# Fewer accumulator groups, evictions written ahead of weight conversions, and Fourier low parts on VectorE

## The chip, the cores and the metric

The kernel runs on one core of one Trainium2 chip. The metric is the device time of one execution in microseconds (us). TensorE (PE) multiplies, and its results land in accumulators (PSUM banks); VectorE (DVE), ScalarE (ACT) and GpSimd (POOL) do elementwise work; SyncE (SP) only issues DMAs.

## The reference

Three parts run one after the other on two batches of 768 tokens with 512 channels: a block attention with decay, a mixer MLP (token MLP, then channel MLP), and a Fourier block with a second channel MLP. All is float32.

```
x  = attention(q, k, v, lam)                      # per head, decay lam
xt = x.transpose(0, 2, 1)
u  = x + (relu(xt @ w_tok1) @ w_tok2).transpose(0, 2, 1)
x  = u + relu(u @ w_ch1) @ w_ch2                  # channel MLP, 512 -> 1536 -> 512   (m = 0)
u  = x + real(fft(fft(x, axis=1), axis=2))
un = (u - mean(u)) / sqrt(var(u) + 1e-6)
out = u + relu(un @ m_w_ch1) @ m_w_ch2            # second channel MLP, 512 -> 2048 -> 512   (m = 1)
```

The weights arrive as 64-bit floats, which the kernel reads as pairs of 32-bit integer words and turns into float32 itself.

## The kernel before

**Products.** Each float32 operand is split into a high part and a low part (what the high part leaves over), and `mm3` (L114 to L118) makes a product of three matmuls: high times high, high times low, low times high. So a product shows as a turn of L116, L117, L118. A high part is an ACT copy, a low part is a subtraction on DVE or POOL.

**Steps of the two channel MLPs.** `run` (L949) goes through a list `todo` of hidden tiles, one a step. `first(u)` makes the tile's first product into one bank `ph`: 12 matmuls of 384 columns. `relu_split` (L484) then makes its high part on ACT (L485) and its low part on DVE (L486), named `hid`. One step later `second` multiplies `hid` by the second weight and adds it to a group of accumulators `ac`: four banks for m = 0 (12 matmuls of 384 columns), three for m = 1 (9 of 512). So on PE `first` of step i stands ahead of `second` of step i - 1, and a `hid` has the time of one `first` to get ready before PE stands still. In names such as ph_1_0_6 the digits are batch, column half and hidden tile.

**Groups.** `units(m, blocks, last_f)` (L676) orders the hidden tiles: for each (tiles, batch) the two column halves, and in a half all tiles of the list. At the last tile of a half the group ends: DVE adds each bank to the residual, four times 128x384 at L494 for m = 0 (`xT`), three times 128x512 at L502 for m = 1 (`u`). Until that is done the next group's `second` can't write the banks. `G1` holds the twelve tiles of m = 0 in four threes.

**Weights.** `convert(n)` (L260) takes n turns on a stream of jobs. A job of two-word weights (512 KB load on SP, L184) takes one ACT pass (L203), four DVE word operations (L222, L223, L225, L226), and then either an ACT copy and a POOL subtraction into one of 16 places of converted weights (L252, L253), or, for a job of kind "ahead" (raw names end in a), a store to a scratch in memory (L234), from where the weight comes back later as float32 (256 KB load, names end in s). A converted place is taken only when one is free (`room`); three buffers hold raw words, three hold the results. `TURNS` says how many turns are taken in a step (1 where it says nothing), and `TURNS_7` how many in the last part.

**Fourier.** Its pieces (`fourier_ab`, `fourier_d`, sums, y, gather, columns, rows, mid, and `norm`) are called from within the steps at half-steps given in `WHEN`. `fourier_y` computes six arrays y (L775 to L795), and `emit` splits each: the unscaled four with an ACT copy (L760) and a POOL subtraction (L761), the two scaled ones on ACT and, put off to the end of the piece in the list `late`, on DVE (L767). They go into `ya` and `yb`, which the column transforms (`pm`) and `fourier_mid` (`pz`, L811 and L812) multiply.

**The last part.** The rest of the second MLP is done by `seven` (L596), which makes two by two blocks of products from seven (`pa`, `pb`, `pc`), with sums of inputs and weights; `between` takes conversion turns and `second_of` between its products.

**Order.** The order on PE and SP is the one that the code is written in. On DVE, ACT and POOL a scheduler orders the instructions from what is written and what waits for what.

## Time and profile before

| | us |
| --- | --- |
| median of 3 runs (632.94 to 635.19) | 634.0 |
| the profiled execution, its own time | 631.0 |
| span of its trace | 629.2 |
| TensorE busy | 600.1 |
| VectorE busy | 465.8 |
| ScalarE busy | 236.5 |
| GpSimd busy | 157.1 |

The profiled execution is one more run beside the three. The trace gives the start and length of each instruction and what its engine waited for last. Times along the trace are counted from the start of the span. The m = 0 MLP runs alone from about 129 us to 264 us, the Fourier transform of the first batch between its last steps to 312 us, then the second batch's with the second MLP to 440 us, and the last part follows.

### The profile page before, as it was taken

Reading aid. Unit: us, or ns where it says so; the run is one execution under the profiler, and the core shown is the slowest. Engines: PE = TensorE matmul, PEld = TensorE weight load, DVE = VectorE, ACT = ScalarE, POOL = GpSimd, SP = SyncE. Lnnn points to the kernel's source line nnn. Section 1 sums busy time; section 2 is a strip of 40 time slices with the busy share of each in tenths; the row PEclk is TensorE's granted clock in tenths of the full one; section 3 lists DMA queues with packets and bytes.
Section 4 is the critical chain, followed back from the end, with each engine's and each line's share of the span. In section 5 each row is a group of like instructions: output and inputs, shape, how many; then the busy total and the mean of one; then the engine's idle time right before and its main releaser. Section 6 shows DMA issues by size and latency. Waiting matters only on the chain. (4 is left out here: it accounts for less than half of the span.)

```text
span 629.2 us, 9565 instructions
## 1 busy us (share of the span) xinstructions
PE 600.1 (95%) x3624; PEld 547.3 (87%) x3624; DVE 465.8 (74%) x894; ACT 236.5 (38%) x480; POOL 157.1 (25%) x127
## 2 busy tenths in 40 slices
PE   9999899999899998999899999999999998999997
PEld 7677699899799997999899899888889977999996
DVE  6799899999978689448786885885697699335335
ACT  2575654534323324134434451323443442221110
POOL 5254223324201401014523440024402332110000
PEclk9999999999999999999999999999999999999999
DMA  8955334414574586201102001003203424000005
GB/s 286 400 219 168 125 101 129 144 68 145 168 251 125 177 262 195 102 0 45 58 18 83 26 10 35 17 1 84 83 2 124 161 68 134 1 0 1 0 1 200
DMA packets 25069, 66.35 MB, mean 105 GB/s; under 512 B 2872, under 2 KB 4032, under 8 KB 25024
## 3 DMA queue, kind: packets, MB, share of 16 engines
q1 hardware_dynamic: 24736, 65.62, 31.5%
q8 instruction: 28, 0.46, 0.3%
q10 hardware_dynamic: 288, 0.14, 0.1%
q14 instruction: 17, 0.14, 0.1%
HBM read 55.51 MB, written 10.23 MB: 104 GB/s over the span
## 5 line engine op out<-in xcount | busy, mean ns | idle before, releaser
L118 PE MATMUL ac<-w_b,hid 128*128 128x512 f32 x192 | 75.9, 395 | 0.3 <-DVE hid L486 0.3
L117 PE MATMUL ac<-w_b,hid 128*128 128x512 f32 x192 | 75.7, 394 | 0.0
L116 PE MATMUL ac<-w_b,hid 128*128 128x512 f32 x192 | 74.9, 390 | 0.0
L116 PE MATMUL ac<-hid,w_b 128*128 128x384 f32 x192 | 64.9, 338 | 4.4 <-DVE xT L494 4.3
L117 PE MATMUL ac<-hid,w_b 128*128 128x384 f32 x192 | 64.8, 338 | 2.7 <-DVE hid L486 2.7
L118 PE MATMUL ph<-uh,w_a 128*128 128x384 f32 x192 | 64.4, 335 | 0.5 <-POOL w_a L253 0.5
L116 PE MATMUL ph<-uh,w_a 128*128 128x384 f32 x192 | 64.6, 337 | 0.0
L118 PE MATMUL ac<-hid,w_b 128*128 128x384 f32 x192 | 64.3, 335 | 0.0
L117 PE MATMUL ph<-uh,w_a 128*128 128x384 f32 x192 | 64.2, 334 | 0.0
L486 DVE SCALAR_TENSOR_TENSOR hid<-ph,hid 128x384 fp32r<-128x384 f32 x68 | 37.5, 551 | 34.4 <-ACT hid L485 34.3
L485 ACT ACTIVATE hid<-ph 128x384 fp32r<-128x384 f32 x68 | 33.0, 486 | 72.2 <-PE ph L118 72.1
L253 POOL TENSOR_TENSOR w_a<-m_a,w_a 128x512 fp32r<-128x512 f32 x17 | 25.1, 1478 | 91.6 <-ACT w_a L252 56.1
L118 PEld LDWEIGHTS ac<-w_b,hid 128*128 128x128 f32 x192 | 36.0, 188 | 8.4 <-DVE hid L486 0.7
L117 PEld LDWEIGHTS ac<-w_b,hid 128*128 128x128 f32 x192 | 36.0, 188 | 6.1
L116 PEld LDWEIGHTS ac<-w_b,hid 128*128 128x128 f32 x192 | 36.1, 188 | 5.8
L116 PEld LDWEIGHTS ac<-hid,w_b 128*128 128x128 f32 x192 | 36.0, 188 | 5.8 <-ACT hid L485 2.4
L117 PEld LDWEIGHTS ac<-hid,w_b 128*128 128x128 f32 x192 | 36.1, 188 | 4.1 <-DVE hid L486 3.9
L253 POOL TENSOR_TENSOR w_b<-m_b,w_b 128x512 fp32r<-128x512 f32 x17 | 24.0, 1410 | 62.2 <-ACT w_b L252 32.5
L118 PEld LDWEIGHTS ph<-uh,w_a 128*128 128x128 f32 x192 | 36.0, 188 | 0.8 <-POOL w_a L253 0.8
L117 PEld LDWEIGHTS ph<-uh,w_a 128*128 128x128 f32 x192 | 36.1, 188 | 0.1
L116 PEld LDWEIGHTS ph<-uh,w_a 128*128 128x128 f32 x192 | 36.1, 188 | 0.1
L118 PEld LDWEIGHTS ac<-hid,w_b 128*128 128x128 f32 x192 | 36.0, 188 | 0.0
(466 smaller groups left out, 1509.6 us busy)
## 6 DMA issues: line engine op xcount, KB each, us to landing
qkv<-qkv SPq DMA_DIRECT2D x7, 768.0 KB, 8.1
single_scratch<-m_a SPq DMA_DIRECT2D x16, 256.0 KB, 4.2
qkv<-qkv SPq DMA_DIRECT2D x10, 384.0 KB, 5.8
kp<-kT SPq DMA_DIRECT2D x8, 384.0 KB, 6.3
single_scratch<-m_b SPq DMA_DIRECT2D x11, 256.0 KB, 4.4
out<-u SPq DMA_DIRECT2D x11, 256.0 KB, 2.0
raw_t_0d<-w_tok SPq DMA_DIRECT2D x2, 384.0 KB, 7.5
raw_t_1d<-w_tok SPq DMA_DIRECT2D x2, 384.0 KB, 3.1
```

The lines of the kernel that those rows point to most:

```text
L116: nc.tensor.matmul(ps, wt[0], xt[0], start=first, stop=False, **kw)
L117: nc.tensor.matmul(ps, wt[0], xt[1], start=False, stop=False, **kw)
L118: nc.tensor.matmul(ps, wt[1], xt[0], start=False, stop=last, **kw)
L253: nc.gpsimd.tensor_tensor(out=t[:, 1, :n], in0=src, in1=f32(t[:, 0, :n]), op=ALU.subtract)
L485: nc.scalar.activation(hi, ps, AF.Relu)
L486: stt(out=lo, in0=ps, scalar=0.0, in1=f32(hi), op0=ALU.max, op1=ALU.subtract)
```

## The change

1. The lists of hidden tiles are cut into fewer, longer groups. For m = 0 there were seven entries with 14 group ends (56 additions at L494): tiles G1[0] for batch 0, then for batch 1, G1[1] for batch 0, then for batch 1, G1[2] with G1[3] for batch 0, G1[2] for batch 1, G1[3] for batch 1. Now there are five entries with 10 ends (40 additions). For m = 1, batch 0, two entries become one: 4 ends with 12 additions become 2 with 6. The number and kind of matmuls stay.
2. At a step whose `second` ends a group, `convert` is called behind `second` and no longer ahead of it, in `run` and in `between`.
3. The low parts of the four unscaled Fourier arrays of each batch (8 operations of 128x512) go from POOL to DVE and are put off to the end of their piece.
4. `TURNS` has other values: no conversion in steps 39 to 42, and two turns at more of the other steps. The first piece of the Fourier transform of batch 0 comes two steps later (half-step 67, not 63).

```diff
-WHEN = ((63, 71, 77, 73, 74, 77, 74, 77, 77, 79, 80, 81, 85, 83, 86, 85, 87, 84, 88, 90, 92, 91, 94, 97, 99),
+WHEN = ((67, 71, 77, 73, 74, 77, 74, 77, 77, 79, 80, 81, 85, 83, 86, 85, 87, 84, 88, 90, 92, 91, 94, 97, 99),
...
-TURNS = {3: 0, 5: 0, 20: 3, 21: 3, 22: 3, 23: 2, 24: 2, 26: 2, 28: 2, 41: 0, 42: 0, 45: 0, 48: 0, 49: 0, 62: 0, 65: 0}
+TURNS = {3: 0, 5: 0, 16: 2, 18: 2, 20: 2, 22: 2, 24: 2, 26: 2, 28: 2, 29: 2, 39: 0, 40: 0, 41: 0, 42: 0, 43: 2, 45: 2, 46: 2,
+         48: 0, 49: 0, 62: 0, 65: 0}
...
                 nc.scalar.activation(yh[:, 0, :], src, AF.Copy)
-                nc.gpsimd.tensor_tensor(out=yh[:, 1, :], in0=src, in1=f32(yh[:, 0, :]), op=ALU.subtract)
+                late.append(lambda: tt(out=yh[:, 1, :], in0=src, in1=f32(yh[:, 0, :]), op=ALU.subtract))
...
-    todo = units(0, [(G1[0], 0), (G1[0], 1), (G1[1], 0), (G1[1], 1), (G1[2] + G1[3], 0), (G1[2], 1), (G1[3], 1)], 11)
-    todo += units(1, [(G1[0], 0), (G1[1], 0)], 15)
+    todo = units(0, [(G1[0], 0), (G1[0] + G1[1], 1), (G1[1] + G1[2], 0), (G1[3], 0), (G1[2] + G1[3], 1)], 11)
+    todo += units(1, [(G1[0] + G1[1], 0)], 15)
...
-            convert(TURNS.get(i, 1))
+
+            ends = i > 0 and todo[i - 1][1] is not None and todo[i - 1][4] == todo[i - 1][1][-1]
+            if not ends:
+                convert(TURNS.get(i, 1))
             for fn, args in side.get(2 * i, []):
                 fn(*args)
             if i > 0:
                 second(todo[i - 1])
+            if ends:
+                convert(TURNS.get(i, 1))
...
-            convert(TURNS_7[j] * (i + 1) // 4 - TURNS_7[j] * i // 4)
-            if pend:
-                pend.pop(0)()
+            turns = TURNS_7[j] * (i + 1) // 4 - TURNS_7[j] * i // 4
+            ends, fn = pend.pop(0) if pend else (False, lambda: None)
+            if ends:
+                fn()
+            convert(turns)
+            if not ends:
+                fn()
```

How the instructions stand on VectorE around the first group end inside the m = 0 stretch; before (the end belongs to batch 1, column half 0; `m_a_9` and `m_b_9` are weights whose words are being converted):

```order
L225 SCALAR_TENSOR_TENSOR m_b_8_1818<-raw_b_8d,m_b_8_1818 128x512
L222 TENSOR_SCALAR m_a_9_1857<-m_a_9_1857 128x512
L226 SCALAR_TENSOR_TENSOR m_b_8_1818<-raw_b_8d,m_b_8_1818 128x512
L486 SCALAR_TENSOR_TENSOR hid_1_1_0_1595<-ph_1_1_0_1582,hid_1_1_0_1595 128x384
L494 TENSOR_TENSOR xT_178<-ac_1_0_0_0_1527,xT_178 128x384
L494 TENSOR_TENSOR xT_178<-ac_1_0_0_1_1528,xT_178 128x384
L494 TENSOR_TENSOR xT_178<-ac_1_0_0_2_1529,xT_178 128x384
L494 TENSOR_TENSOR xT_178<-ac_1_0_0_3_1530,xT_178 128x384
L223 TENSOR_SCALAR m_a_9_1857<-m_a_9_1857 128x512
L222 TENSOR_SCALAR m_b_9_1900<-m_b_9_1900 128x512
L225 SCALAR_TENSOR_TENSOR m_a_9_1857<-raw_a_9d,m_a_9_1857 128x512
L223 TENSOR_SCALAR m_b_9_1900<-m_b_9_1900 128x512
```

and after (the same group now ends three tiles later):

```order
L227 SCALAR_TENSOR_TENSOR m_a_9_1886<-raw_a_9d,m_a_9_1886 128x512
L487 SCALAR_TENSOR_TENSOR hid_1_0_4_1634<-ph_1_0_4_1621,hid_1_0_4_1634 128x384
L487 SCALAR_TENSOR_TENSOR hid_1_0_5_1673<-ph_1_0_5_1660,hid_1_0_5_1673 128x384
L487 SCALAR_TENSOR_TENSOR hid_1_1_0_1712<-ph_1_1_0_1699,hid_1_1_0_1712 128x384
L495 TENSOR_TENSOR xT_178<-ac_1_0_0_0_1527,xT_178 128x384
L495 TENSOR_TENSOR xT_178<-ac_1_0_0_1_1528,xT_178 128x384
L495 TENSOR_TENSOR xT_178<-ac_1_0_0_2_1529,xT_178 128x384
L495 TENSOR_TENSOR xT_178<-ac_1_0_0_3_1530,xT_178 128x384
L223 TENSOR_SCALAR m_b_9_1897<-m_b_9_1897 128x512
L224 TENSOR_SCALAR m_b_9_1897<-m_b_9_1897 128x512
```

The four additions stood directly behind the `hid` before too; what is new is that no word operation stands among the two `hid` ahead of them.

On VectorE in `fourier_y` of batch 0, before:

```order
L783 TENSOR_TENSOR y_3_3048<-q_2591,y_0_3036 128x512
L787 TENSOR_TENSOR y_4_3069<-ra_1_2974,ra_2_2975 128x512
L789 SCALAR_TENSOR_TENSOR y_5_3071<-y_4_3069,ra_0_2973 128x512
L767 TENSOR_TENSOR ya_3034<-y_1s,ya_3034 128x512
L792 TENSOR_TENSOR y_6_3075<-ra_1_2974,ra_2_2975 128x512
L486 SCALAR_TENSOR_TENSOR hid_1_1_8_3099<-ph_1_1_8_3086,hid_1_1_8_3099 128x384
L795 TENSOR_TENSOR y_7_3081<-ra_0_2973,y_4_3069 128x512
L767 TENSOR_TENSOR yb_3035<-y_3s,yb_3035 128x512
```

and after:

```order
L784 TENSOR_TENSOR y_3_3005<-q_2627,y_0_2994 128x512
L762 TENSOR_TENSOR ya_2992<-y_1_2996,ya_2992 128x512
L788 TENSOR_TENSOR y_4_3023<-ra_1_2940,ra_2_2941 128x512
L487 SCALAR_TENSOR_TENSOR hid_1_0_10_2989<-ph_1_0_10_2976,hid_1_0_10_2989 128x384
L768 TENSOR_TENSOR ya_2992<-y_1s,ya_2992 128x512
L762 TENSOR_TENSOR yb_2993<-y_3_3005,yb_2993 128x512
L790 SCALAR_TENSOR_TENSOR y_5_3025<-y_4_3023,ra_0_2939 128x512
L793 TENSOR_TENSOR y_6_3028<-ra_1_2940,ra_2_2941 128x512
L796 TENSOR_TENSOR y_7_3034<-ra_0_2939,y_4_3023 128x512
L762 TENSOR_TENSOR ya_2992<-y_5_3025,ya_2992 128x512
L487 SCALAR_TENSOR_TENSOR hid_1_0_11_3053<-ph_1_0_11_3040,hid_1_0_11_3053 128x384
```

Two of the four low parts per batch (L762) show here among the y; POOL has no instruction between the additions of the batch's `fourier_ab` and its gather any more (before it had the four low parts and five weight conversions there).

A fifth thing follows from the new turns. One pair of weights of the second MLP, a_10 and b_10, is no longer turned to float32 ahead of time. In the last part it is loaded as two-word weights (512 KB, raw_a_10d and raw_b_10d) instead of as float32 (256 KB, raw_a_10s and raw_b_10s), and its word operations stand there. VectorE at the first block of seven (number 2; `u_1_2` is made from the product `pb_2`, `hid_2_11` from `pa_2`), before:

```order
L486 SCALAR_TENSOR_TENSOR hid_1_1_3_4549<-ph_1_1_3_4536,hid_1_1_3_4549 128x384
L613 TENSOR_TENSOR u_1_2_4589<-pb_2_4582,m_1_2_4580 128x384
L486 SCALAR_TENSOR_TENSOR hid_2_11_4606<-pa_2_4573,hid_2_11_4606 128x384
L619 TENSOR_TENSOR v_1_2_4615<-pb_2_4582,m_1_2_4580 128x384
L567 TENSOR_TENSOR x_0_0_4659<-un_0_3389 128x384
```

and after:

```order
L614 TENSOR_TENSOR u_1_2_4527<-pb_2_4520,m_1_2_4518 128x384
L223 TENSOR_SCALAR m_a_10_4713<-m_a_10_4713 128x512
L224 TENSOR_SCALAR m_a_10_4713<-m_a_10_4713 128x512
L226 SCALAR_TENSOR_TENSOR m_a_10_4713<-raw_a_10d,m_a_10_4713 128x512
L227 SCALAR_TENSOR_TENSOR m_a_10_4713<-raw_a_10d,m_a_10_4713 128x512
L487 SCALAR_TENSOR_TENSOR hid_2_11_4544<-pa_2_4511,hid_2_11_4544 128x384
L620 TENSOR_TENSOR v_1_2_4553<-pb_2_4520,m_1_2_4518 128x384
```

The four word operations of a_10 now stand ahead of `hid_2_11` on the engine.

## Rows read from the trace of the kernel before

**Rows 1.** The page: busy us of each engine, share of the span, instructions.
```profile
PE 600.1 (95%) x3624; PEld 547.3 (87%) x3624; DVE 465.8 (74%) x894; ACT 236.5 (38%) x480; POOL 157.1 (25%) x127
```

**Rows 2.** Timeline of PE: start us, us, instruction, [idle before <-what ended it].
```profile
129.16 0.34 PE L116 MATMUL ph<-uh,w_a 128*128 128x384 f32 x1
...
137.49 0.33 PE L116 MATMUL ph<-uh,w_a 128*128 128x384 f32 x1
...
204.04 0.41 PE L116 MATMUL ac<-hid,w_b 128*128 128x384 f32 x1 [0.86 <-DVE xT L494]
...
263.58 0.33 PE L116 MATMUL ph<-uh,w_a 128*128 128x384 f32 x1
```

**Rows 3.** Waits of PE, 129 to 264 us: total us, times, longest us.
```profile
PE ac L116 <- DVE xT L494: 4.3, 4, 1.6
PE ac L117 <- DVE hid L486: 2.7, 3, 1.3
```

**Rows 4.** Timeline of DVE around the group end at 148 us.
```profile
144.42 0.41 DVE L222 TENSOR_SCALAR m_b<-m_b 128x512 f32<-128x512 f32 x1
...
145.33 0.69 DVE L225 SCALAR_TENSOR_TENSOR m_b<-raw_b_8d,m_b 128x512 uint32<-128x512 uint32 x1
145.94 1.54 DVE L222 TENSOR_SCALAR m_a<-m_a 128x512 f32<-128x512 f32 x1
...
148.00 0.55 DVE L486 SCALAR_TENSOR_TENSOR hid<-ph,hid 128x384 fp32r<-128x384 f32 x1
148.47 1.94 DVE L494 TENSOR_TENSOR xT<-ac,xT 128x384 f32<-128x384 f32 x4
```

**Rows 5.** Timeline of POOL around the same group end.
```profile
145.91 1.29 POOL L253 TENSOR_TENSOR w_a<-m_a,w_a 128x512 fp32r<-128x512 f32 x1 [3.03 <-ACT w_a L252]
```

**Rows 6.** Timeline of SP's queue, 215 to 250 us: first and last of ten loads.
```profile
217.81 0.33 SPq L184 DMA_DIRECT2D raw_a_6a<-m_ch  x1
...
242.39 0.33 SPq L184 DMA_DIRECT2D raw_b_10a<-m_ch  x1
```

**Rows 7.** Waits of PE, 264 to 312 us.
```profile
PE pm L117 <- DVE ya L767: 1.6, 1, 1.6
PE pz L811 <- ACT at L841: 1.6, 1, 1.6
```

**Rows 8.** Timeline of DVE in fourier_y of batch 0.
```profile
292.95 1.79 DVE L787 TENSOR_TENSOR y<-ra,ra 128x512 f32<-128x512 f32 x1
295.92 1.77 DVE L789 SCALAR_TENSOR_TENSOR y<-y,ra 128x512 f32<-128x512 f32 x1 [1.18 <-POOL ya L761]
297.61 1.75 DVE L767 TENSOR_TENSOR ya<-y_1s,ya 128x512 fp32r<-128x512 f32 x1
```

**Rows 9.** Waits of PE, 312 to 440 us.
```profile
PE pq L116 <- DVE u L867: 0.6, 1, 0.6
...
PE pn L901 <- DVE unf L892: 0.4, 1, 0.4
```

**Rows 10.** Timeline of DVE in the normalization of batch 1.
```profile
394.55 0.68 DVE L502 TENSOR_TENSOR u<-ac,u 128x512 f32<-128x512 f32 x1
```

**Rows 11.** Timeline of DVE in the last part, blocks 2 and 3.
```profile
446.22 0.56 DVE L613 TENSOR_TENSOR u<-pb,m 128x384 f32<-128x384 f32 x1 [2.54 <-PE pb L118]
449.88 0.56 DVE L486 SCALAR_TENSOR_TENSOR hid<-pa,hid 128x384 fp32r<-128x384 f32 x1 [3.10 <-ACT hid L485]
...
477.37 0.56 DVE L486 SCALAR_TENSOR_TENSOR hid<-pa,hid 128x384 fp32r<-128x384 f32 x1 [2.88 <-ACT hid L485]
```

**Rows 12.** Timeline of SP's queue, block 2.
```profile
444.48 0.32 SPq L180 DMA_DIRECT2D raw_a_10s<-single_scratch  x1
```

**Rows 13.** DMA issues, 440 to 530 us: count, KB each, median us to landing.
```profile
raw_b_11d<-m_ch SPq DMA_DIRECT2D x1, 512.0 KB, 3.5
...
raw_a_10s<-single_scratch SPq DMA_DIRECT2D x1, 256.0 KB, 2.6
```

**Rows 14.** Waits of PE, 440 to 530 us.
```profile
PE pc L116 <- DVE hid L486: 1.2, 2, 1.0
```

More of the change, by code (lines that the diff above doesn't have):

```diff
@@ L1013, in body @@
             input_sums_last(1, k)
-        pend = [lambda: second(todo[-1])]
+        pend = [(False, lambda: second(todo[-1]))]
         place = {"i": 0}
@@ L1033, in body @@
             else:
-                pend.extend([lambda x=x: second_of(*x) for x in todo_])
+                pend.extend([(x[4], lambda x=x: second_of(*x)) for x in todo_])
             if j < 2:
```

## The prediction

> **What bounds the kernel now.** I read the page's busy times first: TensorE is at work in 600.1 us, 95% of the span [rows 1], and the change leaves its matmuls as they are. So what it can win is where TensorE stands still, and what it can lose is a new stop. I looked for the stops stage by stage.
>
> In the m = 0 MLP the timeline gives the length of an undisturbed step: two steps from 129.16 to 137.49 us, so 4.165 us each [rows 2]. The thirty steps from 129.16 to 263.58 us took 134.42 us and should have taken 30 x 4.165 = 124.95: 9.5 us are lost. The list of waits of that stretch names 4.3 us behind the additions of group ends (L494) and 2.7 us behind low parts of hidden tiles (L486) [rows 3], 7.0 in all. The other 2.5 are restarts and stops too short for the list, so a listed us stands for 9.5 / 7.0 = 1.35 lost ones, a factor that I use below. Both waits are on VectorE, which runs late here. The reader sees why in the 148 us rows [rows 4]: word operations stand up to the hidden tile's low part at 148.00, the first two of them run at full speed, and one that should take 0.41 takes 1.54, because the POOL subtraction that starts at 145.91 runs beside it [rows 4, 5]: 1.1 us for one such meeting. Then four additions take 1.94 more.
>
> In the Fourier transform of batch 0 TensorE waits twice for 1.6 us [rows 7]. VectorE stands behind a POOL low part (1.18 idle before 295.92), and its own operations there take 1.75 to 1.79 instead of 0.69 [rows 4, 8].
>
> **m = 0, steps 6 to 35 (term A).** Ends of groups in this stretch go from 8 to 6, since the ends after steps 9, 15 and 21 go and one after step 33 comes. Two ends less are two times 1.94 us of VectorE [rows 4]; more matters what stands around them. Counted in the order of the new kernel, no word operation stands in the two steps ahead of the end at 12 (the fence in the section on the change shows it) and none in steps 24 to 27, so these ends meet a VectorE without a backlog. Those at 30 and 33 have 19 word operations in three steps and then 13. A job's four cost 1.52 us for the first three (144.42 to 145.94) and 0.61 for the fourth, taken as the third's pitch, so 2.13 or 0.53 each [rows 4]. 19 x 0.53 and three low parts of 0.47 (148.00 to 148.47) make 11.5 of the 12.5 us of three steps: no backlog either.
>
> What is left is steps 14 to 23, which take 61 word operations now and one end (at 18). That is 61 x 0.53 + 10 x 0.47 + 1.94 = 39.0 us of 41.65. The nearest stretch before is steps 13 to 21: 41 word operations and three ends, 41 x 0.53 + 9 x 0.47 + 3 x 1.94 = 31.8 of 37.5, and its largest stop is the one at 204.04, 0.86 idle [rows 2], about 1.2 lost. The new stretch leaves 2.7 us of spare time where that one had 5.7. Loads and the buffers of results may set the pace as well: ten loads of such weights were issued between 217.81 and 242.39, 24.58 / 9 = 2.73 us a job [rows 6], and 61 operations are 15.25 jobs, so 41.6 us. It just fits. A hidden tile's low part can be ready some 1.2 us after its product (an ACT pass, taken as 0.6, and its own 0.55 [rows 4]) and is asked for 4.2 us, one step, later, so 3.0 us of lateness cost nothing (an estimate from these). I keep 2.5 us of the 9.5, double the old stretch's stop, and take **A = -7.0**. Ends: -9.3, if only a short stop stays; -3.5, if the full 3 us of missing spare time are lost behind the end and again behind POOL meetings of 1.1 us.
>
> The second edit, evictions ahead of conversions, I cost at nothing: the additions already followed the low part at once (148.00, then 148.47 [rows 4]), and the order shows no other place for them.
>
> **Fourier of batch 0 (term B).** The two waits of 1.6 [rows 7] are 3.2 x 1.35 = 4.3 us. POOL leaves the chain, so the 1.18 idle and the stretching by 1.1 of some four operations (292.95, 295.92, 297.61 and the next [rows 8]) go: 5.6 us off a chain that was late by 1.6 at `pm` and, on top of that, by 1.6 at `pz`. VectorE takes four low parts more, each at most 0.69 like the word operation at 145.33 [rows 4], 2.8 us, of which two stand ahead of the last array for `pm`. In addition the end after step 39 is gone, whose four additions took 1.94 together. 5.6 - 2.8 + 1.9 is more than the 3.2 needed, so both stops go: **B = -4.3**, between -3.2 (bare waits) and, in a rival, nothing. Batch 1 has no such stop, and its four low parts (2.8 us) lie beside full steps: 0.
>
> **Second MLP (term C).** The end after step 45 is gone, whose 1.94 us stood ahead of the chain to `u` (L867), for which `pq` waits 0.6; and the three additions of 0.68 (the last at 394.55 [rows 10]) no longer stand in the chain to `unf`, for which `pn` waits 0.4 [rows 9]. 1.0 x 1.35 = 1.4 at most, 0 at least; **C = -1.0**.
>
> **a_10 and b_10 (term E, a cost).** In block 2 VectorE now has the four word operations of a_10 ahead of `hid_2_11`. The load's issue stood at 444.48 [rows 12] and stays there; 512 KB land in 3.5 us where 256 KB took 2.6 [rows 13], so at 448.0. The ACT pass, taken as 0.6 us, ends at 448.6, the four operations 2.13 later at 450.7, and the low part starts there instead of at 449.88 [rows 11]. TensorE waits for just this low part already (`pc` behind `hid`, 1.2 us in two waits [rows 14]), so all is passed on: +0.8. POOL's subtraction of a sum of weights falls there, and one meeting costs 1.1: **E = +1.9**. Upper end +3.5, with a second meeting and the landing half a us later. The operations of b_10 fit in the 2.88 idle ahead of 477.37 [rows 11]: 2.13 hidden, 0, up to +2.1 were that cover gone. Other stops of the last part stay.
>
> **Sum.** -7.0 - 4.3 - 1.0 + 1.9 = -10.4 us. The profiled execution took 631.0, so a profiled one after should take 620.6. It lay 3.0 under the median of the three runs, 634.0, and the difference should be the same there: **623.6**.
>
> **The rivals.** *First, the crowd in steps 14 to 23 eats the gain.* If a job takes 3.5 us there instead of 2.73, by POOL meetings and uneven loads, 15.25 x 3.5 = 53.4 us stand against 41.65 and 3.0 of lateness: 8.7 lost, A = -0.8, in all -4.2, so 629.8. For it speaks that 4.3 of the 7.0 listed us came where word operations stand around ends [rows 3], against it that 2.73 was kept under the same buffers with stops in it. 0.14.
>
> *Second, slower.* The same place, worse: loads, three buffers and VectorE in turn take 4.0 us a job, and every hidden tile of ten steps comes late. 61.0 - 41.65 - 3.0 = 16.4 lost, A = +6.9, in all +3.5: 637.5. It decides from 3.9 us a job, where A = +5.2 and the sum is over +1.8. No mean of several jobs before was near it. 0.07.
>
> *Third, the low parts load VectorE.* Its four more operations of 0.69 take the place of POOL's on the path to `pm` and `pz`, and the stops stay: B = 0, in all -6.1, 627.9; if all 2.8 come on top, 630.7. For it speaks that VectorE is already the late engine, against it the 1.18 idle behind POOL in this very chain [rows 8]. 0.11.
>
> On this last one the Trainium skill, "Perfetto Trace Analysis", Optimizing Scalar/DVE Operations, speaks against the change: where VectorE is saturated, work may be handed to ScalarE or even GpSimd, and the change hands it the other way. The same sentence adds that GpSimd and VectorE share an SBUF read port, so that moving work between the two may not help. The trace bears out the second half at 145.94: there the pair running together is what costs. By the first half the result would be 627.9 to 630.7, by the second 623.6.
>
> *That the change doesn't do what it says* holds for its second edit, which moves nothing on VectorE and is in the sum at 0.
>
> **How the numbers follow.** Forecast 0.68, rivals 0.14, 0.07 and 0.11. The ends of the terms make -9.3 - 4.3 - 1.4 + 0.8 = -14.2 (619.8) and -3.5 - 3.2 + 0 + 3.5 + 2.1 = -1.1 (632.9), not likely all at once. With 1 us for the scatter of a median, the range is 618.5 to 630.0; it takes in the first and nearly all of the third rival and leaves out the second and the worst ends. About 0.3%, 1.9 us, is what a measurement of this kernel can tell from no change: the same is 632.1 to 635.9. Faster by more: nearly all of the forecast and most of the first and third rival, 0.88; the same 0.05; slower 0.07.
>
> **What would show it.** In the trace after: the thirty steps to `ph_1_0_6` take 127.5 us, and what is lost lies between steps 14 and 24 (A right), or more is lost there (first and second rival). No wait of `pm` and `pz` in the Fourier stage, and single y operations at 0.69 (B), or `pm` behind a low part on VectorE (third). `pc` of block 2 waits about 2 us longer behind `hid` (E). I am wrong in the mechanism if the gain lies in other places, or if TensorE waits for a converted weight from POOL.

## The result and the profile after

The kernel after takes 627.74 us (median of four runs, 624.14 to 630.07) against 634.6 us before in the same session; the ratio is 0.989, with a 95% interval of 0.9847 to 0.9934. The forecast was 623.6, so the direction and the range held and a third of the forecast gain is missing: 6.9 us came of the 10.4.

| | before | after |
| --- | --- | --- |
| median, us | 634.6 | 627.74 |
| the profiled execution, its own time | 631.0 | 629.25 |
| span of its trace | 629.2 | 627.5 |

The two profiled executions are only 1.7 us apart, and the reason lies outside the change. I cut each trace at seven starts of TensorE products that both programs share. The cuts are the first product of step 6 of the m = 0 stretch (`ph_1_0_0`), that of step 36 (`ph_1_0_6`), the first of the second MLP, and the first of blocks 2, 3 and 7 of the last part. A block has the number of its pair of hidden tiles, and from 3 on both batches have one, so "blocks 3 to 6" are eight blocks. Each number is the difference of two starts in the timeline of PE, in us:

| kernel | to step 6 | thirty steps | Fourier | second MLP | block 2 | blocks 3 to 6 | rest |
| --- | --- | --- | --- | --- | --- | --- | --- |
| before | 129.16 | 134.42 | 77.66 | 102.61 | 10.99 | 130.71 | 43.65 |
| after | 132.49 | 131.65 | 74.05 | 102.74 | 14.02 | 128.93 | 43.62 |
| difference | +3.33 | -2.77 | -3.61 | +0.13 | +3.03 | -1.78 | -0.03 |

Up to step 6 the instructions on all five engines stand in the same order in both programs; the 3.3 us there are scatter between executions (the last section comes back to it). From step 6 on the profile gives -5.0 us, where the medians give -6.9; what the other 1.9 are, one profile of each can't tell. The experiments below are read by the same table.

The waits of PE in the thirty steps, after (engine, line, what it waited for: us in total, times, longest), which answer [rows 3]:

```profile
PE ac L118 <- DVE hid L487: 2.3, 3, 1.4
PE ac L117 <- DVE xT L495: 1.5, 2, 0.9
```

The listed waits behind group ends fell from 4.3 to 1.5 us, those behind low parts of hidden tiles from 2.7 to 2.3. In the Fourier stretch the list of waits that had the two of 1.6 us [rows 7] is empty after. From 312 to 440 us it reads:

```profile
PE pq L117 <- DVE mv L883: 0.8, 1, 0.8
...
PE pu L860 <- DVE un L909: 0.5, 1, 0.5
...
PE pn L902 <- DVE unf L893: 0.4, 1, 0.4
```

Where [rows 9] had `pq` behind `u` for 0.6 and `pn` behind `unf` for 0.4, `pn` waits as before, `pq` waits for the statistics of the normalization instead, and `pu` is a new wait. Nothing was won there.

Block 2 of the last part, after, on SP's queue, ACT, DVE and POOL (start us, us, instruction, [idle before <- what ended it]), which answers [rows 11, 12]:

```profile
441.50 0.33 SPq L185 DMA_DIRECT2D raw_a_10d<-m_ch  x1
```

```profile
444.65 0.67 ACT L204 ACTIVATE m_a<-raw_a_10d 128x512 f32<-128x512 f32 x1 [1.97 <-DMA raw_a_10d<-m_ch]
```

```profile
445.35 0.43 DVE L223 TENSOR_SCALAR m_a<-m_a 128x512 f32<-128x512 f32 x1 [1.49 <-ACT m_a L204]
445.81 0.43 DVE L224 TENSOR_SCALAR m_a<-m_a 128x512 uint32<-128x512 uint32 x1
446.27 1.67 DVE L226 SCALAR_TENSOR_TENSOR m_a<-raw_a_10d,m_a 128x512 uint32<-128x512 uint32 x1
447.97 1.64 DVE L227 SCALAR_TENSOR_TENSOR m_a<-raw_a_10d,m_a 128x512 uint32<-128x512 uint32 x1
449.53 0.55 DVE L487 SCALAR_TENSOR_TENSOR hid<-pa,hid 128x384 fp32r<-128x384 f32 x1
```

```profile
446.07 1.32 POOL L245 TENSOR_TENSOR w_s<-raw_s_4s,w_s 128x512 fp32r<-128x512 f32 x1 [4.60 <-issue]
447.57 1.49 POOL L245 TENSOR_TENSOR w_s<-raw_s_4s,w_s 128x512 fp32r<-128x512 f32 x1 [0.18 <-ACT w_s L244]
```

This is the predicted cost, near its upper end. The load comes in, the four operations of a_10 start, and two of them, not one, meet a POOL subtraction: 1.67 and 1.64 us where 0.69 is usual. The Trainium skill, "SBUF — State Buffer", Who interferes with whom, has VectorE and GpSimd share a port pair that one of them holds for a whole instruction; the rows agree: both word operations end 0.55 us after the end of the POOL subtraction beside them (447.39 and 449.06), as if most of their 0.69 us had come only then. What follows on PE:

```profile
450.13 0.44 PE L117 MATMUL pc<-tops,w_s 128*128 128x384 f32 x1 [2.75 <-DVE hid L487]
450.41 0.34 PE L118 MATMUL pc<-tops,w_s 128*128 128x384 f32 x1
450.58 0.34 PE L119 MATMUL pc<-tops,w_s 128*128 128x384 f32 x1
...
451.54 0.52 PE L117 MATMUL pb<-un,w_a 128*128 128x384 f32 x1
451.86 0.52 PE L118 MATMUL pb<-un,w_a 128*128 128x384 f32 x1
452.18 0.52 PE L119 MATMUL pb<-un,w_a 128*128 128x384 f32 x1
```

After the 2.75 us of standing still the next matmuls start every 0.17 us, then for some ten matmuls every 0.32: the granted clock fell to its lower level (1.2 GHz) for about 3 us (its mean from 448 to 456 us was 0.79). I had not counted that.

### The profile page after: what moved, and what is told of

It reads as the page before. It is cut to its first block, busy times and chain, and to the rows that moved or that the text cites. A ratio compares the mean times of both kernels' runs of the same rounds, so it can differ in the third digit from the quotient of the medians.

```text
span 627.5 us, 9527 instructions
## 1 busy us (share of the span) xinstructions
PE 602.4 (96%) x3624; PEld 550.2 (88%) x3624; DVE 458.1 (73%) x880; ACT 236.1 (38%) x480; POOL 145.2 (23%) x119
## 5 line engine op out<-in xcount | busy, mean ns | idle before, releaser
L254 POOL TENSOR_TENSOR w_a<-m_a,w_a 128x512 fp32r<-128x512 f32 x18 | 26.3, 1461 | 103.5 <-ACT w_a L253 102.2
L254 POOL TENSOR_TENSOR w_b<-m_b,w_b 128x512 fp32r<-128x512 f32 x18 | 25.5, 1416 | 66.5 <-ACT w_b L253 37.2
```

What stands on the lines that cost most here:

```text
L254: nc.gpsimd.tensor_tensor(out=t[:, 1, :n], in0=src, in1=f32(t[:, 0, :n]), op=ALU.subtract)
```

## The experiments

"Theory" in the expectations is what I held before the run. The first four separate the parts, the next four test what these said, the last four try to mend what is left.

### The low parts on VectorE alone

```diff
 # the kernel before, in emit:
-                nc.gpsimd.tensor_tensor(out=yh[:, 1, :], in0=src, in1=f32(yh[:, 0, :]), op=ALU.subtract)
+                late.append(lambda: tt(out=yh[:, 1, :], in0=src, in1=f32(yh[:, 0, :]), op=ALU.subtract))
```

> The kernel before with the third edit alone: the four unscaled low parts of each batch on VectorE, at the end of their piece; groups, turns and order of calls as before, so POOL still converts weights (w_b_0, w_a_1, w_b_1) beside the chain. Theory: the POOL low parts in the chain are what made pm and pz late, so both waits of 1.6 us go and the time falls by about 4 us, ratio 0.994. Rival: the conversions left on POOL stretch the low parts on VectorE from 0.69 to 1.8, four of them 4.4 us, and the waits stay at 1 to 2 us each: no change within 1 us, ratio 0.999 to 1.002.

Measured: 637.96 us, ratio 1.0014 (0.9985 to 1.0043). The Fourier stretch took 78.96 us, 1.3 more than before. The waits of PE there:

```profile
PE pz L811 <- ACT at L841: 1.7, 1, 1.7
PE pz L812 <- DVE yb L761: 1.6, 1, 1.6
```

and two rows of DVE in the chain:

```profile
297.95 1.78 DVE L761 TENSOR_TENSOR ya<-y,ya 128x512 fp32r<-128x512 f32 x1
...
301.96 1.77 DVE L761 TENSOR_TENSOR yb<-y,yb 128x512 fp32r<-128x512 f32 x1
```

`pm` is in time now, but `pz` waits 1.7 and then 1.6 us, and the second of these is for one of the moved low parts. POOL goes on converting weights, and a low part on VectorE meets that as a low part on POOL did. Behind the second wait the clock fell (0.73 from 309 to 313 us), which makes some 1.6 of the 78.96 us; without it the stretch would be near 77.4 (an estimate from the lengths of the same products before), still 3.3 above the changed kernel. The rival held: the third edit alone wins nothing.

### The groups alone

```diff
 # the kernel before:
-    todo = units(0, [(G1[0], 0), (G1[0], 1), (G1[1], 0), (G1[1], 1), (G1[2] + G1[3], 0), (G1[2], 1), (G1[3], 1)], 11)
-    todo += units(1, [(G1[0], 0), (G1[1], 0)], 15)
+    todo = units(0, [(G1[0], 0), (G1[0] + G1[1], 1), (G1[1] + G1[2], 0), (G1[3], 0), (G1[2] + G1[3], 1)], 11)
+    todo += units(1, [(G1[0] + G1[1], 0)], 15)
```

Since `WHEN` stays, the first Fourier piece of batch 0 reads the residual of a column half before the tiles of G1[3] are added to it. This kernel so leaves these tiles out of a part of the transform; the amount of work is the same.

> The kernel before with the new lists of hidden tiles alone (10 group ends for 14 and 2 for 4), turns as before. Theory: ends meet VectorE's conversions wherever the turns put them, so fewer ends alone win only what two ends less in the 30 steps are worth, 1.5 to 3 us of the 9.5 lost there, and the pair a_10, b_10 is decided by the turns; ratio 0.995 to 0.998. Rival: the groups are the whole gain of the change in the m = 0 stretch, or more, since the new turns crowd steps 14 to 23: 3 to 6 us less lost there, ratio 0.990 to 0.995.

Measured: 636.4 us, ratio 0.9982 (0.9951 to 1.0013): nothing that can be told from no change, the theory's upper edge. But the table shows two large parts that cancel: the thirty steps take 138.70 us, 4.3 more than before, and the Fourier stretch 74.04, 3.6 less, the whole of the change's gain there, with the low parts still on POOL. In the thirty steps two stops of 2.2 and 2.0 us were followed by a fall of the clock, and cost 4.0 and 3.8 us. The new lists need the new turns, and the Fourier gain comes with the lists and not with the low parts; a kernel below that leaves nothing out repeats it.

### a_10 and b_10 converted ahead again

```diff
 # the changed kernel:
-... 28: 2, 29: 2, 39: 0, ...
+... 28: 2, 29: 2, 31: 2, 33: 2, 39: 0, ...
```

> The changed kernel with two more turns (two instead of one at steps 31 and 33), so that a_10 and b_10 of the second MLP are converted ahead again and loaded as 256 KB float32 in the last part. Theory: the wait of pc in block 2 falls from 2.9 us to 0.4, its clock stays at the upper level, and the stretch from the first product of block 2 to the first of block 3 goes from 14.0 to 11.0 us; 3 us less than the changed kernel, ratio to before about 0.984. Rival: the two jobs cost as much where they now stand (steps 31 to 34, where a group ends after 33): no change against 0.989, with new stops of 2 to 3 us between 245 and 264 us.

Measured: 630.06 us, ratio 0.9893 (0.9858 to 0.9927), no gain over the changed kernel. Block 2 did what the theory says: 10.99 us. The thirty steps took 133.90, 2.25 more than in the changed kernel. A stop at 180 us, no longer than there (1.34 against 1.36), had a fall of the clock behind it and cost 1.5 more, and new stops at the end of the stretch cost 2.4, while others were shorter; the waits of PE from 240 to 270 us were 0.7 in the changed kernel and are now:

```profile
PE ac L118 <- DVE hid L487: 1.2, 1, 1.2
PE ac L117 <- DVE xT L495: 1.2, 2, 0.8
```

And blocks 3 to 6 took 131.57 us, 2.6 more than in the changed kernel. So both were true: the wait in block 2 goes, and about as much is lost elsewhere. The fall of the clock need not be the jobs' doing: the same stop stands in nine other kernels without one.

### Four buffers for the words

```diff
 # the changed kernel:
-BUFS = {"raw": 3, "man": 3, "hid": 4, "half": 5, "t": 9}
+BUFS = {"raw": 3, "man": 4, "hid": 4, "half": 5, "t": 8}
```

> The changed kernel with four buffers instead of three for the words being converted; to make room, eight instead of nine temporaries for the Fourier part. In the changed kernel jobs of steps 17 to 23 started every 3.23 us (ten between 179.61 and 211.87), and VectorE waited for the ACT pass, which waited for a store to free a buffer. Theory: these buffers set the pace; with four the jobs go at 2.4 to 2.7 us, and the thirty steps from ph_1_0_0 to ph_1_0_6 take 127 to 129.5 us instead of 131.65; 2 to 4 us less than the changed kernel unless the missing temporary costs some in the Fourier part. Rival: VectorE's own work and its meetings with POOL set the pace: 131 to 132 us as it was.

Measured: 633.67 us, ratio 0.9947 (0.9914 to 0.9981). The thirty steps took 133.20. The jobs' passes on ACT from `raw_b_1a` to `raw_b_11d` took 31.52 us for ten, 3.15 each against 3.23, and the passes now wait for loads:

```profile
205.43 0.66 ACT L204 ACTIVATE m_a<-raw_a_11d 128x512 f32<-128x512 f32 x1 [0.85 <-DMA raw_a_11d<-w_ch]
208.80 0.66 ACT L204 ACTIVATE m_b<-raw_b_5a 128x512 f32<-128x512 f32 x1 [2.71 <-DMA raw_b_5a<-m_ch]
210.74 0.67 ACT L204 ACTIVATE m_b<-raw_b_11d 128x512 f32<-128x512 f32 x1 [0.89 <-DMA raw_b_11d<-w_ch]
```

The theory fell: the fourth buffer moved the wait from the store to the load and the pace by 0.08 us a job. A stop of 2.3 us at the group end, with a fall of the clock behind it, cost 4.1 us (1.1 in the changed kernel), and the run also loses time ahead of step 6 (the clock, and a longer wait for a weight at 99 us), so its total says little about the buffer. Its block 2 took 12.66 us, and the part on the prediction comes back to that.

### The order of calls as it was

```diff
 # the changed kernel, in run and likewise in between:
-            if not ends:
-                convert(TURNS.get(i, 1))
+            convert(TURNS.get(i, 1))
 ...
-            if ends:
-                convert(TURNS.get(i, 1))
```

> The changed kernel without its second edit: conversions are called ahead of the evictions at group ends again. Theory (as predicted): the additions follow the hidden tile's low part on VectorE either way, so nothing moves: ratio to before as the changed kernel's 0.989, within 0.003, and the m = 0 stretch within 1 us of 131.65. Rival: conversions slip between at one end in four, 1 to 2 us more in that stretch.

Measured: 626.77 us, ratio 0.9848 (0.9809 to 0.9887); thirty steps 132.13, Fourier 74.05. The second edit is worth nothing, as predicted.

### The low parts back on POOL

```diff
 # the changed kernel, in emit:
-                late.append(lambda: tt(out=yh[:, 1, :], in0=src, in1=f32(yh[:, 0, :]), op=ALU.subtract))
+                nc.gpsimd.tensor_tensor(out=yh[:, 1, :], in0=src, in1=f32(yh[:, 0, :]), op=ALU.subtract)
```

> The changed kernel with the four unscaled low parts per batch on POOL again. The prediction's theory: POOL in the chain of y is what made pm and pz late, so the stretch from ph_1_0_6 to the second MLP's first product goes from 74.05 back by 2 to 4 us to 76 to 78, and the time by as much. Theory now, from the kernels with the low parts alone (78.96) and the groups alone (74.04): the gain came with the longer last group of m = 0, which keeps all places of weights taken, so that POOL converts nothing there and no additions stand in step 39; the low parts' engine is worth nothing: 73.9 to 74.6.

Measured: 627.26 us, ratio 0.9864 (0.9822 to 0.9905), and 74.05 us for the Fourier stretch, to the hundredth that of the changed kernel. POOL in that stretch:

```profile
289.58 1.61 POOL L762 TENSOR_TENSOR ya<-y,ya 128x512 fp32r<-128x512 f32 x1 [18.78 <-ACT ya L761]
...
297.57 1.29 POOL L762 TENSOR_TENSOR yb<-y,yb 128x512 fp32r<-128x512 f32 x1 [1.91 <-ACT yb L761]
...
304.25 1.29 POOL L254 TENSOR_TENSOR w_a<-raw_a_0s,w_a 128x512 fp32r<-128x512 f32 x1 [3.93 <-ACT w_a L253]
```

POOL makes its four low parts between 289 and 299 us and converts the first weight of the second MLP (`w_a`, L254) only at 304. In [rows 8] VectorE stood 1.18 us behind such a low part; in the trace of before, POOL had a conversion right ahead of that low part, and VectorE ran against both:

```profile
292.37 1.82 POOL L253 TENSOR_TENSOR w_b<-raw_b_0s,w_b 128x512 fp32r<-128x512 f32 x1 [2.86 <-ACT w_b L252]
294.15 1.74 POOL L761 TENSOR_TENSOR ya<-y,ya 128x512 fp32r<-128x512 f32 x1
```

Without the conversion the low part on POOL is early enough.

### One merged entry of the list

```diff
 # the kernel before:
-    todo = units(0, [..., (G1[2] + G1[3], 0), (G1[2], 1), (G1[3], 1)], 11)
+    todo = units(0, [..., (G1[2] + G1[3], 0), (G1[2] + G1[3], 1)], 11)
```

> The kernel before with one edit: the last two entries of the m = 0 list, G1[2] and G1[3] for batch 1, are one. Nothing else of the change. Theory: this alone brings the Fourier gain: the stretch from ph_1_0_6 to the second MLP's first product falls from 77.66 to 74.0, the m = 0 stretch ahead of it stays at 134 to 135 (plus up to 1.5 where the clock falls), the last part stays; ratio 0.993 to 0.995. Rival: the low parts on VectorE are needed as well, and 1.6 us of the two stops stay: 75.5 to 76.5, ratio 0.997.

Measured: 630.03 us, ratio 0.9911 (0.9881 to 0.994). The Fourier stretch took 74.02 us, the thirty steps 134.47, block 2 10.98: one line of the list brings all of the Fourier gain, and from step 6 on no other stretch moves by more than 0.6 us. Its interval (0.9881 to 0.994) lies almost wholly within that of the whole change (0.9847 to 0.9934), so that the rest of the change wins anything in the whole is not shown. Why the line does it, as far as the code and the trace say: with one long list for G1[2] and G1[3] in batch 1 all weights of both are needed until the second column half. The 16 places stay taken, so `room` lets no weight of the second MLP in until step 42, POOL has nothing to convert beside y (its first `w_a` of the second MLP comes at 305.84 us, where before it came at 288.21), and no group ends after step 39. Which of the two, the conversions or the end's 1.94 us, weighs more no run here tells apart.

### Fewer word operations in steps 19 to 23

```diff
 # the changed kernel:
-TURNS = {3: 0, 5: 0, 16: 2, 18: 2, 20: 2, 22: 2, ... 28: 2, 29: 2, 39: 0, ...
+TURNS = {3: 0, 5: 0, 14: 0, 16: 0, 18: 0, 20: 1, 22: 2, ... 28: 2, 29: 2, 31: 2, 33: 2, 39: 0, ...
```

> The changed kernel with fewer turns at steps 14 to 20 and more at 31 and 33: VectorE then has 3, 2, 0, 0, 0 word operations in steps 19 to 23 instead of 4, 6, 6, 7, 6 (as ordered), and two pairs of second-MLP weights less are converted ahead, so more two-word loads in the last part. Theory: word operations that wait for loads stand ahead of the hidden tiles' low parts and make the stops at 205 and 215 us (1.0 and 0.5 us lost) and part of the one at 193 (1.1); they go, and the m = 0 stretch takes 129.5 to 130.5 instead of 131.65, while the stop of 2.2 us at 177 stays; the last part gets 2 to 6 us longer. Rival: these stops come with the group end at step 18, and stay as they are.

Measured: 632.01 us, ratio 0.9945 (0.9913 to 0.9978). The stops that were at 205 and 215 us (1.0 and 0.5 us lost) are gone, the one behind the end at 18 lost 0.8 and not 1.1, and the one of 2.2 stayed. But stops of 1.3 and 1.4 us came at 255 and 259, where the jobs went, and the thirty steps took 132.92. The last part paid as expected: block 2 alone took 16.98. The theory is right that word operations make the stops at 205 and 215 and wrong on the sum: the jobs have to stand somewhere. What these operations wait for is not a load but, in the changed kernel's trace, a store that frees a buffer.

### Word operations behind low parts in the last part

```diff
 # the changed kernel, in relu_split and in convert:
-        stt(out=lo, in0=ps, scalar=0.0, in1=f32(hi), op0=ALU.max, op1=ALU.subtract)
+        on_act["lo"] = stt(out=lo, in0=ps, scalar=0.0, in1=f32(hi), op0=ALU.max, op1=ALU.subtract).ins
...
                 for op in word_ops():
-                    op()
+                    with (tc.issue_after(on_act["lo"]) if step["i"] >= 68 else nullcontext()):
+                        op()
```

`issue_after` sets the order on the engine and adds no wait.

> The changed kernel with one tie in the last part: word operations go on VectorE behind the latest low part of a hidden tile that the code has reached, so a_10's stand behind hid_2_11 and no longer ahead of it. Theory: a_10's place on VectorE is the whole cost in block 2: the wait of 2.75 us of pc goes to under 0.5, the fall of the clock behind it goes too, and the stretch from the first product of block 2 to that of block 3 goes from 14.0 to 10.9 to 11.3 us; the later blocks stay within 1 us. About 3 us less than the changed kernel, ratio 0.982 to 0.986. Rival: the POOL subtractions of w_s_4 or the ACT order hold hid_2_11 back as well, 12.5 to 13.5 us stay; or the words, now later, make a weight late for block 5 by as much.

Measured: 630.63 us, ratio 0.9943 (0.9916 to 0.997). Block 2 took 9.84 us, even less than before the change. But the rival came true later, in block 6:

```profile
PE pb L117 <- ACT w_s L244: 4.2, 1, 4.2
PE pb L119 <- POOL w_s L245: 2.1, 1, 2.1
```

A sum of weights was 6 us late, the clock fell behind the wait, and blocks 3 to 6 took 135.44 us.

### The same tie from step 13 on

```diff
-                    with (tc.issue_after(on_act["lo"]) if step["i"] >= 68 else nullcontext()):
+                    with (tc.issue_after(on_act["lo"]) if step["i"] > 12 else nullcontext()):
```

> The same tie from step 13 on, so in the m = 0 stretch too: word operations stand behind the low part of their own step and are spread over steps 14 to 38, where the changed kernel has them crowded ahead of hidden tiles (up to 8 between two). Theory: what is left of the stops in that stretch comes from word operations that wait for loads ahead of a low part; the stops at 177, 187, 193, 205 and 215 (5.2 us lost in all) shrink to under 2, and the stretch takes 127 to 129 us instead of 131.65; with block 2 mended some 6 us less than the changed kernel, ratio 0.978 to 0.982. Rival: VectorE has too little spare time whatever the order, and the stops come elsewhere in the stretch: 131 to 133.

Measured: 644.1 us, ratio 1.0136 (1.0086 to 1.0187), slower than before. The thirty steps took 139.66 us:

```profile
PE ac L118 <- DVE hid L488: 5.8, 5, 2.7
PE ac L117 <- DVE xT L496: 4.0, 2, 2.8
```

The stop at 177 is gone, but steps 19 to 35 lost 14.8 us. The rival held, and by more than its 131 to 133: spreading the operations doesn't make them fewer, and the stops come elsewhere and longer. Blocks 3 to 6 took 139.37 us, with the same late sum of weights as in the run before.

### TensorE kept busy through a wait

```diff
 # the changed kernel, in EARLY, and a new act v that makes 16 transposes of ident into a free bank:
-... u6 s7 u7 r6 o00
+... u6 s7 v u7 r6 o00
```

> The changed kernel with 16 transposes of a constant (128x128) put on TensorE into the wait of about 2 us ahead of the last attention states (66 us); they compute nothing that is used. In some profiles the granted clock of 66 to 82 us is 1.00, in others 0.68 to 0.89, always behind this wait, and the stretch up to the m = 0 MLP takes 129.2 to 136.3 us. Theory: the clock falls because TensorE stood still; with the wait filled it stays at 1.00, the stretch takes 129 to 130.5, and the median falls by 1 to 3 us against the changed kernel, with a narrower spread. Rival: the clock falls without regard to this wait: no change of median or spread, 0.7 to 0.9 in some profile.

Measured: 627.23 us, ratio 0.9866 (0.9826 to 0.9905). Two rows of the windows view, 66 to 82 us (us; busy us of PE, PEld, DVE, ACT and POOL with counts; granted clock; DMA share; GB/s), first the changed kernel:

```profile
66.00:82.00 16.00, 14.02 (x108) 10.73 (x106) 12.33 (x31) 10.30 (x23) 2.56 (x2) 0.89 0.24 82
```

and this one:

```profile
66.00:82.00 16.00, 15.10 (x118) 12.14 (x120) 12.98 (x29) 10.48 (x23) 3.13 (x3) 0.89 0.28 97
```

The mean clock is the same. But the transposes did not fill the wait:

```profile
66.90 2.39 PE L1003 MATMUL warm<-ident 128*128 128x128 f32 x16 [2.29 <-DVE st L385]
```

They wait themselves, 2.29 us, for VectorE to be done with the bank that they write, so TensorE stood still for as long as in the changed kernel (1.85 us). The theory was not tested, and what decides there stays open. The median is that of the changed kernel; the six runs lie within 1.9 us, for which no cause is shown. The run helped in another way: its block 2 had the a_10 operations and no fall of the clock, and took 12.00 us where three other kernels with them and with a fall (the changed one, and those with the old order of calls and the low parts on POOL) took 14.0 to 14.4. Only one of its four operations met POOL, though, and `pc` waited 1.3 us and not 2.7 to 3.1.

### The tie for a_10 alone

```diff
-                    with (tc.issue_after(on_act["lo"]) if step["i"] >= 68 else nullcontext()):
+                    with (tc.issue_after(on_act["lo"]) if jobs[at_["word"] - 1] == ("double", ("a", 1, 10)) else nullcontext()):
```

> The changed kernel with the tie for one job alone: the four word operations of a_10 in the last part stand on VectorE behind the low part of hid_2_11 (they come after hid_2_12, beside those of a_11); every other conversion stands where the changed kernel has it. Theory: the stretch from the first product of block 2 to that of block 3 goes from 14.0 us to 9.8 to 11.0, as with the tie for all, and the later blocks keep their conversions in time: 80 to 83 us from block 3 to block 7 (81.8 in the changed kernel), no wait of pb in block 6 for a sum of weights. 3 us less than the changed kernel, ratio 0.980 to 0.985. Rival: the delayed job makes the ones behind it late, and a wait of 2 us or more for w_s or w_b in blocks 5 or 6 gives the gain back: 0.986 to 0.990.

Measured: 626.08 us, ratio 0.9839 (0.9803 to 0.9876). Block 2 took 10.96 us and blocks 3 to 6 129.54. (The 80 to 83 us of the expectation end at the block of batch 0 and number 6, the seventh in order: 82.42 against 81.81 in the changed kernel.) DVE in block 2:

```profile
445.47 0.56 DVE L615 TENSOR_TENSOR u<-pb,m 128x384 f32<-128x384 f32 x1 [2.53 <-PE pb L119]
449.13 0.56 DVE L488 SCALAR_TENSOR_TENSOR hid<-pa,hid 128x384 fp32r<-128x384 f32 x1 [3.10 <-ACT hid L487]
```

These are the two rows of before again [rows 11]: nothing stands ahead of `hid_2_11`. No wait for a sum of weights came. This is the lowest ratio of the study, but its interval overlaps that of the changed kernel (0.9847 to 0.9934) and of the two kernels with an edit undone (0.9848 and 0.9864), so the 3 us are shown in block 2 and not in the whole.

## Why the prediction was right in direction and a third off in size

That a third and not a half is missing is in part luck. The terms that I had summed to -10.4 came to -3.2 in the profile; -1.8 came where I had forecast nothing, and the medians show 1.9 more than the profile.

**A, thirty steps: -7.0 forecast, -2.8 in the profile** (six kernels with the new lists and turns there took 131.15 to 132.29, three with the old ones 134.42, 134.46 and 135.95; the means are 3.1 apart), outside the term's own ends. The lost time lies where I said, 5.3 of 6.7 us in steps 14 to 24, but it is more. The step that failed is the pace of the jobs there. I took 2.73 us a job from when ten loads were issued in another stretch [rows 6] and found that it "just fits". The ACT passes of these same loads in the trace of before were eight jobs of 3.01 us:

```profile
221.09 0.67 ACT L203 ACTIVATE m_a<-raw_a_6a 128x512 f32<-128x512 f32 x1 [2.61 <-DVE m_a L226]
...
245.17 0.68 ACT L203 ACTIVATE m_a<-raw_a_10a 128x512 f32<-128x512 f32 x1 [1.98 <-DVE abt L697]
```

I had read the pace from the loads, which run ahead of the work. Even at 3.01 the first rival's formula loses only 1.3 us, and in the new steps the passes were slower still:

```profile
179.61 0.69 ACT L204 ACTIVATE m_b<-raw_b_1a 128x512 f32<-128x512 f32 x1 [1.97 <-POOL w_b L254]
...
195.31 0.66 ACT L204 ACTIVATE m_a<-raw_a_4a 128x512 f32<-128x512 f32 x1 [2.44 <-DMA single_scratch<-m_b]
...
211.87 0.67 ACT L204 ACTIVATE m_b<-raw_b_11d 128x512 f32<-128x512 f32 x1 [2.15 <-DMA single_scratch<-m_a]
```

Ten jobs took 32.26 us, 3.23 each. Put into the first rival's formula this gives 15.25 x 3.23 - 41.65 - 3.0 = 4.6 us lost; the five stops from 177 to 215 us lost 2.2 + 0.4 + 1.1 + 1.0 + 0.5 = 5.2. So it was nearest to the first rival, at a milder pace than the 3.5 that I priced, though that the sums agree so well is luck, since the five stops are not of one kind. The one at 205 looks like this on DVE:

```profile
204.47 0.43 DVE L223 TENSOR_SCALAR m_a<-m_a 128x512 f32<-128x512 f32 x1 [1.75 <-ACT m_a L204]
...
206.00 0.55 DVE L487 SCALAR_TENSOR_TENSOR hid<-ph,hid 128x384 fp32r<-128x384 f32 x1
```

VectorE is not short of time here; it stands 1.75 us with a word operation at its head whose data are late, and the low part that TensorE needs is behind it. The lighter turns removed this stop and the one at 215 and put them elsewhere, and four buffers only moved the wait to the loads.

The largest stop, 2.2 us at 177, is another matter:

```profile
176.06 0.68 ACT L204 ACTIVATE m_a<-raw_a_1a 128x512 f32<-128x512 f32 x1 [1.68 <-POOL w_a L254]
176.65 0.47 ACT L486 ACTIVATE hid<-ph 128x384 fp32r<-128x384 f32 x1
...
178.36 0.55 DVE L487 SCALAR_TENSOR_TENSOR hid<-ph,hid 128x384 fp32r<-128x384 f32 x1
...
178.97 0.44 PE L118 MATMUL ac<-hid,w_b 128*128 128x384 f32 x1 [1.36 <-DVE hid L487]
```

On ACT a pass that waits 1.68 us for a POOL subtraction stands ahead of the tile's high part. On VectorE, which works here without a pause, eight word operations stand between this low part and the one before, two of them stretched beside POOL from 0.43 us to 1.31 and 1.51. This stop stayed with the lighter turns and with four buffers, and went only where the tie put word operations behind low parts. I had added up VectorE's work and its pace, not its order.

**B, Fourier: -4.3 forecast, -3.6 measured, for a wrong reason.** The two waits went as forecast (-4.1 by their starts), and 0.5 us came back at `pu` and `pq` in the same stretch. But I put the gain down to POOL leaving the chain by the third edit. That edit alone gave nothing, taken back it cost nothing, and one merged entry of the list gave all. So the size came out near by luck. I saw in the order that POOL had neither low parts nor conversions there, and credited the first. (The fence in the section on the change shows three of the four low parts among the y, not two as said under it.) The conversions had a row of their own in the trace of POOL, and `room` says when they can start. On the rule of the Trainium skill that I weighed ("Perfetto Trace Analysis", Optimizing Scalar/DVE Operations): what came agrees with its second half, that moving work between GpSimd and VectorE may not help, since moving these low parts won nothing in either direction. I had set 623.6, a time with a gain by just that move, beside this half, and it doesn't speak for it.

**C, second MLP: -1.0 forecast, +0.1 measured.** The `pq` half lies in the table's Fourier stretch, in the 0.5 us just named. In the `pn` half the three additions left the queue, and `pn` waits 0.4 as before. They had not been in the chain; behind them VectorE stood waiting for TensorE's own `pm` already before:

```profile
398.00 0.75 DVE L845 TENSOR_TENSOR z<-at,pm 128x256 f32<-128x256 f32 x2 [0.16 <-PE pm L118]
```

After, the same operation waits 0.42 us there. Taking an operation off an engine's queue shortened no wait.

**E, a_10: +1.9 forecast, +3.0 measured.** The mechanism was right, and the price near the upper end for a reason that wasn't in it. Two operations met POOL, not one, and the clock fell behind the wait. The kernel with four buffers shows the two apart: it had both meetings and a longer wait, but matmuls went on every 0.17 us, and block 2 took 12.66:

```profile
455.44 0.44 PE L117 MATMUL pc<-tops,w_s 128*128 128x384 f32 x1 [2.97 <-DVE hid L487]
455.72 0.34 PE L118 MATMUL pc<-tops,w_s 128*128 128x384 f32 x1
455.89 0.34 PE L119 MATMUL pc<-tops,w_s 128*128 128x384 f32 x1
```

So the lateness costs 1.7 with two meetings (12.66 against 10.99) and 1.0 with one (12.00), less than the 1.9 that I had for one, since waits that stood later in the block before went with it; the fall of the clock adds 1.4 (14.02 against 12.66). I had also misread [rows 14]: of its 1.2 us only 0.2 stood in block 2.

**Not forecast: blocks 3 to 6, -1.8.** I had taken them as unchanged. The gain goes with the late conversion: the kernels with a_10 converted ahead take 130.7 to 131.6 us there, those with the late one 128.1 to 129.5 (130.1 with eight temporaries, and 135 and 139 where the tie delayed other jobs). Which operation makes room there stays open. Net of this, the late pair costs 1.2 us and not 3.0, which is part of why converting it ahead again won nothing.

The second edit was rightly put at nothing. The second rival (slower) was far: a pace of 3.9 us was its condition, 3.23 came. The stops of the third rival stayed only in the kernel with the third edit alone.

## What to carry to other kernels

When an edit moves work off an engine at the same time as the program's resource limits (here 16 places of weights) move other work away, test the two apart before crediting either; here the one-line merge brought the whole Fourier gain that I had put down to another edit. On an engine with a fixed order, sum up not only how long its work takes but what stands at the head of its queue and whether its data are there: an operation whose data are late holds up the ready one behind it (1.75 us of VectorE standing still at 205, 1.0 of it lost on TensorE). And a pace read in one stretch is a forecast for that stretch only.

## What the runs showed of the hardware

The granted clock of TensorE scatters between executions of the same instructions. From 66 to 82 us, where before, the changed kernel and the one with the tie for a_10 stand alike, it was 1.00, 0.89 and 0.68 in their profiles, behind waits of 1.86, 1.85 and 2.00 us, and the way to step 6 took 129.16, 132.49 and 134.19 us: nearly as much as the change wins. Stops elsewhere show the same: behind one of 2.75 us at 450 us in the changed kernel TensorE took, after a few matmuls, 0.32 instead of 0.17 us for each of about ten, and behind one of 2.97 with four buffers it did not; behind the stop of 1.35 us at 177 to 182 us it did so in the kernel with two more turns and in none of nine others. So a stop can cost some 1.5 us more than its length, what decides is not shown, and one profile of each kernel can't carry a difference of a few us; cutting the traces at common products could.
